# Turning K with VectorE's 32x32 block transposes, loaded one head per 32 partitions, in a decode attention kernel

## The chip, the cores and the metric

The kernel runs on one core of a Trainium2 chip. The metric is device time in microseconds (us) for one execution. Before the change it is 199.75 us (median of 3 runs, 199.69 to 199.76).

## What is computed

A layer norm of x (8 rows of 512) feeds two branches. One is decode attention with 32 query heads over 8 KV heads; only the last W = 2048 of 8192 cache positions count. The other is a gated MLP. The result is x + attention * silu(MLP).

```python
B, Sq, D = 8, 1, 512
Hq, Hkv, Sk, Dh = 32, 8, 8192, 128          # W = 2048, rep = Hq // Hkv = 4
q = (xn @ wq).reshape(B, Sq, Hq, Dh)
k = repeat(k_cache[:, :, Sk - W:, :], rep);  v = repeat(v_cache[:, :, Sk - W:, :], rep)
p = softmax(einsum("bhqd,bhkd->bhqk", q, k) * Dh ** -0.5)
s = einsum("bhqk,bhkd->bhqd", p, v).reshape(B, Sq, Hq * Dh) @ wo
g = silu((sigmoid(xn @ w_gate) * (xn @ w_up)) @ w_down)      # w_gate, w_up: 512 x 1792
return x + s * g
```

All tensors are bf16. K and V of the window are 33.55 MB each; wq and wo 4.19 MB each; the three MLP weights 1.84 MB each.

## The kernel before

**Tiles.** A unit of work is one tile of K or V: one batch and a group of GL = 4 KV heads, so NT = 16 tiles of each. A tile is 128 partitions x 64 positions x 128 of head dimension in bf16, 2 MB, 16 KB contiguous per partition. Line 109 (`load_kv`) loads it in one transfer, with the four heads interleaved: partition 4p + j holds head j, positions 64p to 64p + 63. K and V use the same function.

**Transfers.** All bulk loads go out on SP's queue (line 87), into a ring of RING = 9 buffers of equal size; wq takes two of them at first. The list `loads` (line 137) orders the tiles by the slot that needs them: K tile i at slot 4i, V tile i at slot 4i + PV_LAG, with PV_LAG = 11. The three MLP weights stand before the last two V tiles, and wo comes last. `issue_loads` issues as many as there are free buffers; each issue waits on SP for the former user of its buffer.

**Slots.** The order of work is written by hand (line 597). A slot t is a quarter of a K tile (16 of its 64 positions per partition, CC = 16); there are 8 slots for a batch and 64 in all. `k_half` (line 406) runs twice a slot. It reads K as 32-bit words (two neighbouring bf16 of the head dimension) and turns 128x128 words on TensorE against a 32-bit identity, four to a PSUM bank (line 415); VectorE copies the bank to `kT_sb` in SBUF and sorts the four heads apart on the way (line 419). So after every second slot, `kT_sb` holds 64 word indices x 2 positions on its partitions. `qk` (line 423) then makes the scores: 2 halves of the word (e) x 4 heads, each head a product with 32 columns of weights in its own 32 columns of the array (line 434), summed over the batch's 8 slots into one PSUM bank. The query weights come from `qz_sb` (line 262), a zero padded tile; the window that a product reads from it puts the queries in the rows that belong to the slot.

**Queries.** `q_projection` (line 348) makes q in two halves, with the head dimension's even and odd members apart; ScalarE copies it to bf16 (line 369), VectorE turns 32x32 blocks (line 371) and places it into `qz_sb` with 32 copies of 32 elements (line 376).

**Softmax and PV.** Once a batch: row maximum (446), exponent on ScalarE (460), a VectorE block transpose (474), a permutation by TensorE (480) that brings the probabilities from head-major to the interleaved order of V's partitions, a copy, four masked copies (496), and the denominator (518, 520). `pv` (line 525) follows PV_LAG slots behind with 8 products a slot, and a sum for each tile (557, 564). At the end come the MLP (line 629), the output product with wo (line 647), gate and residual.

Of the kernel before, what the change touches and what calls it, by code (L numbers as in the profile page):

```python
# [10 lines left out]
def kernel(  # L11
# [13 lines left out]
    nc = tc.nc  # L25
    P = 128
    B, _, D = A_x.shape
    _, Hkv, Sk, Dh = A_k_cache.shape
    Hq = A_wq.shape[1] // Dh
    rep = Hq // Hkv  # L30
# [4 lines left out]
    win0 = Sk - W  # L35
# [2 lines left out]
    ALIGN = 512  # L38


    GL = 4
    NG = Hkv // GL
    PP = P // GL
    CH = W // PP
    NJ = 4
    CC = CH // NJ
    HALF = CC // 2
    NX = NG * NJ
    XR = NX * rep
    NT = B * NG  # L50
    SPB = NG * NJ
    NSLOT = B * SPB
    PV_LAG = SPB + 3

    D2 = Dh // 2
    NJ2 = NJ // 2
    QB = 2 * rep
    QPAD = XR - QB
    RING = 9
    NCOL = 2  # L60
    DC = D // NCOL

    bf16 = mybir.dt.bfloat16
    f32 = mybir.dt.float32
# [6 lines left out]
    consts = ctx.enter_context(tc.tile_pool(name="consts", bufs=1))  # L71
    work = ctx.enter_context(tc.tile_pool(name="work", bufs=1))
    small = ctx.enter_context(tc.tile_pool(name="small", bufs=2))
    ring = ctx.enter_context(tc.tile_pool(name="ring", bufs=RING))
    ktpool = ctx.enter_context(tc.tile_pool(name="ktpool", bufs=2))
    ppool = ctx.enter_context(tc.tile_pool(name="ppool", bufs=2))
    psum = ctx.enter_context(
        tc.tile_pool(name="psum", bufs=2, space=bass.MemoryType.PSUM)
# [8 lines left out]
    def load(dst, src, q=None):  # L87
        if q is None:
            q = nc.sync
        q.dma_start(out=dst, in_=src)  # L90

    def ring_tile(shape, name):
        return ring.tile(shape, bf16, name=name, tag="ring", align_bytes=ALIGN)
# [5 lines left out]
    KH = KT // 2  # L99
    wq_sb = []  # L100
# [5 lines left out]
    k_tiles = {}  # L106
    v_tiles = {}

    def load_kv(cache, i, name):
        b, gg = divmod(i, NG)  # L110
        t = ring_tile([P, CH, Dh], name)
        load(
            t[:].rearrange("p c d -> p (c d)"),
            cache[b, GL * gg : GL * (gg + 1), win0:Sk, :].rearrange(
                "j (p c) d -> p j (c d)", c=CH
            ),
        )
        return t

    wg_sb = []  # L120
# [42 lines left out]
    def issue_loads():  # L163
        while loads_done[0] < len(loads) and free_bufs[0] > 0:
            kind, i = loads[loads_done[0]]
            if kind == 0:
                k_tiles[i] = load_kv(A_k_cache, i, "k_sb")
            elif kind == 1:
                v_tiles[i] = load_kv(A_v_cache, i, "v_sb")
            elif kind == 2:  # L170
                load_mlp(i)
            else:
                load_wo(i)
            loads_done[0] += 1
            free_bufs[0] -= 1
# [10 lines left out]

    ident = consts.tile([P, P], bf16, name="ident")
    make_identity(nc, ident[:])
    identf = consts.tile([P, P], f32, name="identf")
    make_identity(nc, identf[:])  # L190
    SumM = consts.tile([P, P], f32, name="SumM")
    nc.gpsimd.memset(SumM[:], 0.0)
    for off in range(-rep * (NJ - 1), rep * NJ, rep):
# [64 lines left out]

    QW = 3 * QPAD + 2 * QB
    qz_sb = work.tile([P, B, Hkv, QW], bf16, name="qz_sb")
    nc.vector.memzero(qz_sb[:])


# [32 lines left out]
    FQ = F // 4  # L298
# [2 lines left out]
    gate = work.tile([NCOL * 32, DC], f32, name="gate")  # L301

    def unit_in(w_sb):
        d_ps = psum.tile([P, FQ], f32, name="d_ps", tag="kT_ps")
        for kt in range(KT):
            for c in range(4):
                nc.tensor.matmul(
                    d_ps[32 * c : 32 * (c + 1), :],
                    lhsT=xnT_sb[:, kt, :],
                    rhs=w_sb[:, kt, FQ * c : FQ * (c + 1)],  # L310
                    start=(kt == 0),
                    stop=(kt == KT - 1),
                    tile_position=(0, 32 * c),
                    skip_group_check=True,
                )
        d_tiles.append(d_ps)
# [29 lines left out]


    def q_projection():
        HH = Hq // 2
        q_ps = [  # L350
            psum.tile([P, HH, 32], f32, name=f"q_ps{hh}", tag="kT_ps") for hh in range(2)
        ]
        for kt in range(KT):
            for hh in range(2):
                for c in range(4):
                    nc.tensor.matmul(  # L356
                        q_ps[hh][32 * c : 32 * (c + 1), :, :],
                        lhsT=xnT_sb[:, kt, :],
                        rhs=wq_sb[kt // KH][:, kt % KH, :].rearrange(
                            "p (h a m e) -> p h a m e", a=2, m=32, e=2  # L360
                        )[:, HH * hh : HH * (hh + 1), c % 2, :, c // 2],
                        start=(kt == 0),
                        stop=(kt == KT - 1),
                        tile_position=(0, 32 * c),
                        skip_group_check=True,
                    )
        for hh in range(2):
            q_sb = ppool.tile([P, HH * 32], bf16, name="q_sb", tag="p_bf")
            nc.scalar.copy(out=q_sb[:], in_=q_ps[hh][:].rearrange("p h m -> p (h m)"))
            qT_sb = ppool.tile([P, HH * 32], bf16, name="qT_sb", tag="pt_bf")  # L370
            nc.vector.transpose(out=qT_sb[:], in_=q_sb[:])  # L371
            GH = Hkv // 2
            for e in range(2):
                for c2 in range(2):
                    for r in range(rep):
                        nc.vector.tensor_copy(  # L376
                            out=qz_sb[
                                D2 * c2 : D2 * (c2 + 1),
                                :,
                                GH * hh : GH * (hh + 1),  # L380
                                QPAD + (QB + QPAD) * e + rep * c2 + r,
                            ],
                            in_=qT_sb[D2 * e : D2 * (e + 1), :].rearrange(
                                "p (g r b) -> p r b g", r=rep, b=32
                            )[:, r, :B, :],
                        )

    q_projection()
    free_bufs[0] += 2
# [10 lines left out]
    acc_sbs = {}  # L400
    oT_sb = work.tile([P, B, Hq], bf16, name="oT_sb")

    CP = CC // 2
    HP = CP // 2

    def k_half(t, h2):
        kw = k_tiles[t // NJ][:].rearrange("p (u c) d -> p u (c d)", c=2).bitcast(f32)
        u0 = (t % NJ) * CP + h2 * HP  # L410
        if t % 2 == 0 and h2 == 0:
            kT_tiles[t // 2] = ktpool.tile([P, 2 * CP, GL, PP], f32, name="kT_sb")
        kT_ps = psum.tile([P, HP, P], f32, name="kT_ps")
        for uu in range(HP):
            nc.tensor.transpose(  # L415
                out=kT_ps[:, uu, :], in_=kw[:, u0 + uu, :], identity=identf[:, :]
            )
        o0 = (t % 2) * CP + h2 * HP
        nc.vector.tensor_copy(  # L419
            out=kT_tiles[t // 2][:, o0 : o0 + HP, :, :],  # L420
            in_=kT_ps[:].rearrange("p u (k gl) -> p u gl k", gl=GL),
        )

    def qk(n):
        i, j2 = divmod(n, NJ2)
        b, gg = divmod(i, NG)
        x = NJ2 * gg + j2
        if x == 0:
            s_tiles[b] = psum.tile([P, CC * PP], f32, name="s_ps")
        kT = kT_tiles.pop(n)[:].bitcast(bf16).rearrange("p u gl (k e) -> p u gl k e", e=2)  # L430
        for e in range(2):
            z0 = QPAD + (QB + QPAD) * e - QB * x
            for gl in range(GL):
                nc.tensor.matmul(  # L434
                    s_tiles[b][XR * gl : XR * (gl + 1), :],
                    lhsT=qz_sb[:, b, GL * gg + gl, z0 : z0 + XR],
                    rhs=kT[:, :, gl, :, e],
                    start=(x == 0 and e == 0),
                    stop=(x == NG * NJ2 - 1 and e == 1),
                    tile_position=(0, XR * gl),  # L440
                    skip_group_check=True,
                )

# [33 lines left out]
    def soft_permute(b):  # L477

        pT_ps = psum1.tile([P, CC * XR], f32, name="pT_ps", tag="pT_ps")
        nc.tensor.matmul(  # L480
            pT_ps[:],
            lhsT=perm[:],
            rhs=pt_tiles.pop(b)[:].rearrange("k (u x w) -> k x u w", x=NX // 2, w=QB),
            start=True,
            stop=True,
        )
        pc_bf = ppool.tile([P, CC * XR], bf16, name="pc_bf")
        nc.scalar.copy(out=pc_bf[:], in_=pT_ps[:])  # L488
        pc_tiles[b] = pc_bf
# [107 lines left out]
    for t in range(NSLOT + PV_LAG):  # L597
# [1 line left out]
        b, ph = t // SPB - 1, t % SPB  # L599
        in_b = 0 <= b < B  # L600
        if t < NSLOT:
            k_half(t, 0)
        if in_b and ph == 3:
            soft_mask(b)
            dh_of[b] = soft_den_part(b)
        if t < NSLOT:
            k_half(t, 1)
        if in_b and ph == 2:
            soft_turn(b)
        if 0 < t <= NSLOT and t % 2 == 0:  # L610
            qk(t // 2 - 1)
        if in_b and ph == 0:
            mj_of[b] = soft_max_part(b)
        if in_b and ph == 1:
# [25 lines left out]
    o_rows(1)  # L640


    a_ps = psum.tile([NCOL * 32, DC], f32, name="a_ps", tag="kT_ps")
    order = [(hg, j) for hg in range(HG) for j in range(4)]
    for n, (hg, j) in enumerate(order):
        for c in range(NCOL):
# [48 lines left out]
```

## Time and profile before

| what | before |
|---|---|
| median of 3 runs | 199.75 us |
| the profiled execution | 199.84 us |
| its span, first to last instruction | 198.1 us |
| TensorE busy | 145.6 us, 73% |
| weight loads busy | 99.7 us, 50% |
| VectorE busy | 125.3 us, 63% |
| ScalarE busy | 22.9 us, 12% |
| GpSimd busy | 9.0 us, 5% |
| moved by DMA | 81.26 MB, 410 GB/s over the span |
| issue to landing, K tile and V tile (median) | 32.2 us and 34.9 us |

Engine times overlap, and their shares are means over the whole span. A group of instructions in the profile has its line, engine, operation, output and input tile, shapes and count; then busy time in us, the mean of one in ns; then the engine's idle time just before them and what ended most of it. The DMA share is the mean over the core's 16 DMA engines. Times on TensorE are modelled from start to end and overlap, so the mean of one product is longer than the distance between two.

### The profile page before, as it was taken

How to read it: one execution, taken by the hardware profiler on the slowest of the kernel's cores; microseconds unless marked ns; L12 is line 12 of the kernel's file. 1: busy time of each engine (PE TensorE's matmuls, PEld its weight loads, DVE VectorE, ACT ScalarE, POOL GpSimd, SP SyncE). 2: the span in 40 equal slices, each digit the busy share in tenths (PEclk: the TensorE clock that was granted, in tenths of full speed). 3: DMA queues.
4: the chain of work that ended last, by engine and by line, in shares of the span. 5: the costliest groups of instructions: out<-in, count | busy, mean ns of one | idle time of the engine just before them, and what ended most of it. 6: DMA issues, size and time to landing. Idle time of an engine off the chain costs nothing.

```text
span 198.1 us, 3706 instructions
## 1 busy us (share of the span) xinstructions
PE 145.6 (73%) x1576; PEld 99.7 (50%) x1576; DVE 125.3 (63%) x280; ACT 22.9 (12%) x48; POOL 9.0 (5%) x22
## 2 busy tenths in 40 slices
PE   0073599839997996969696879786949797746682
PEld 0023455526755764657564656564636565325471
DVE  2808867966797788847775867577627787134111
ACT  2001000040021002001100200030000300610000
POOL 7910000000000000000000000000000000000000
PEclk9999999996999999997999979997885999797579
DMA  6999999999999999999999999999999999999970
GB/s 213 425 433 437 440 430 422 423 423 440 433 433 430 427 423 430 427 437 427 433 427 422 437 430 433 427 430 427 427 430 433 431 428 428 435 423 413 418 306 15
DMA packets 6720, 81.26 MB, mean 410 GB/s; under 512 B 776, under 2 KB 816, under 8 KB 1968
## 3 DMA queue, kind: packets, MB, share of 16 engines
q1 hardware_dynamic: 6608, 81.01, 96.3%
q8 instruction: 12, 0.20, 0.4%
q14 instruction: 4, 0.03, 0.0%
q0 software_dynamic: 64, 0.01, 0.0%
q10 hardware_dynamic: 32, 0.01, 0.0%
HBM read 81.02 MB, written 0.01 MB: 409 GB/s over the span
## 4 chain that ended last, share of the span: by engine, by line
DMA 62%; PE 24%; DVE 10%; ACT 1%; issue 1%; SPq 0%; ACTq 0%
DMA k_sb<-in_A_k_cache_dram 31%; DMA v_sb<-in_A_v_cache_dram 18%; PE kT_ps L415 15%; DMA wo_sb<-in_A_wo_dram 7%; DMA wq_sb<-in_A_wq_dram 6%; PE s_ps L434 4%; DVE kT_sb L419 4%; PE acc_ps L536 3%; DVE qz_sb L376 2%; DVE pT_sb L496 1%; PE q_ps L356 1%; DVE qT_sb L371 1%; DVE pt_bf L474 1%; ACT L460 1%; PE den_ps L518 1%
## 5 line engine op out<-in xcount | busy, mean ns | idle before, releaser
L419 DVE COPY kT_sb<-kT_ps 128x512 f32<-128x512 f32 x128 | 83.8, 687 | 34.4 <-PE kT_ps L415 32.5
L415 PE MATMUL kT_ps<-identf,k_sb 128*128 128x128 f32 x512 | 79.1, 300 | 15.0 <-DMA k_sb<-in_A_k_cache_dram 11.3
L415 PEld LDWEIGHTS kT_ps<-identf,k_sb 128*128 128x128 f32 x512 | 61.9, 153 | 38.6 <-issue 20.6
L536 PE MATMUL acc_ps<-v_sb,pT_sb 128*32 128x256 bf16 x512 | 26.8, 298 | 9.5 <-DVE pT_sb L496 8.1
L434 PE MATMUL s_ps<-kT_sb,qz_sb 128*32 128x512 bf16 x256 | 21.9, 422 | 0.3 <-DVE kT_sb L419 0.3
L536 PEld LDWEIGHTS <-pT_sb 128*32 128x32 bf16 x512 | 11.6, 100 | 19.5 <-DVE pT_sb L496 9.0
L549 ACT COPY acc_sb<-acc_ps 128x256 f32<-128x256 f32 x16 | 5.9, 372 | 70.5 <-PE acc_ps L536 70.5
L460 ACT ACTIVATE p_bf<-s_ps,nm 128x512 bf16<-128x512 f32 x8 | 5.5, 687 | 46.4 <-DVE nm L457 46.4
L557 PE MATMUL oT_ps<-Sel,acc_sb 128*128 128x16 f32 x64 | 9.4, 261 | 2.0 <-ACT acc_sb L549 1.1
L557 PEld LDWEIGHTS oT_ps<-Sel,acc_sb 128*128 128x128 f32 x64 | 9.2, 208 | 3.2 <-ACT acc_sb L549 2.0
L496 DVE TENSOR_SCALAR pT_sb<-pc_bf,Hm 128x512 bf16<-128x512 bf16 x32 | 9.0, 346 | 0.0
L480 PE MATMUL pT_ps<-pt_bf,perm 128*128 128x512 bf16 x8 | 3.2, 403 | 7.4 <-DVE pt_bf L474 7.4
L290 PE MATMUL xnT_ps<-ident,xn_bf 8*128 8x8 bf16 x4 | 0.3, 175 | 9.6 <-DVE xn_bf L280 9.6
L434 PEld LDWEIGHTS <-qz_sb 128*32 128x32 bf16 x256 | 4.1, 97 | 6.5 <-issue 6.5
L474 DVE STREAM_TRANSPOSE pt_bf<-p_bf 128x512 bf16<-128x512 bf16 x8 | 5.6, 704 | 1.7 <-ACT p_bf L460 1.7
L647 PE MATMUL a_ps<-wo_sb,o_sb 128*32 128x256 bf16 x64 | 5.5, 329 | 0.9 <-DMA wo_sb<-in_A_wo_dram 0.9
L446 DVE TENSOR_REDUCE mx<-s_ps 128x1 f32<-128x512 f32 x8 | 5.5, 685 | 1.1 <-PE s_ps L434 0.9
L520 DVE RECIPROCAL rden<-den_ps 128x32 f32<-128x32 f32 x8 | 2.9, 358 | 4.4 <-PE den_ps L518 4.4
L194 POOL TENSOR_SCALAR_AFFINE_SELECT SumM<-SumM 128x128 f32<-128x128 f32 x7 | 5.4, 772 | 0.5
L488 ACT CAST pc_bf<-pT_ps 128x512 bf16<-128x512 f32 x8 | 4.7, 585 | 6.4 <-PE pT_ps L480 6.4
L647 PEld LDWEIGHTS <-o_sb 128*32 128x32 bf16 x64 | 4.3, 117 | 1.9 <-issue 1.5
L564 DVE TENSOR_TENSOR oT_sb<-oT_ps,rden 128x16 bf16<-128x16 f32 x16 | 2.7, 166 | 4.0 <-PE oT_ps L557 4.0
(63 smaller groups left out, 60.0 us busy)
## 6 DMA issues: line engine op xcount, KB each, us to landing
k_sb<-in_A_k_cache_dram SPq DMA_DIRECT2D x16, 2048.0 KB, 32.2
v_sb<-in_A_v_cache_dram SPq DMA_DIRECT2D x16, 2048.0 KB, 34.9
wq_sb<-in_A_wq_dram SPq DMA_DIRECT2D x2, 2048.0 KB, 9.7
wo_sb<-in_A_wo_dram SPq DMA_DIRECT2D x2, 1024.0 KB, 31.4
wg_sb<-in_B_w_gate_dram SPq DMA_DIRECT2D x1, 1792.0 KB, 34.0
wu_sb<-in_B_w_up_dram SPq DMA_DIRECT2D x1, 1792.0 KB, 36.4
wd_sb<-in_B_w_down_dram SPq DMA_DIRECT2D x1, 1792.0 KB, 31.3
wo_sb<-in_A_wo_dram SPq DMA_DIRECT2D x3, 512.0 KB, 24.1
```

The costliest lines, as they stand in the source:

```text
L194: nc.gpsimd.affine_select(out=SumM[:], in_=SumM[:], compare_op=ALU.not_equal, fill=1.0, base=-off, pattern=[[-1, P]], channel_multiplier=1,)
L415: nc.tensor.transpose(out=kT_ps[:, uu, :], in_=kw[:, u0 + uu, :], identity=identf[:, :])
L419: nc.vector.tensor_copy(out=kT_tiles[t // 2][:, o0 : o0 + HP, :, :], in_=kT_ps[:].rearrange("p u (k gl) -> p u gl k", gl=GL),)
L434: nc.tensor.matmul(s_tiles[b][XR * gl : XR * (gl + 1), :], lhsT=qz_sb[:, b, GL * gg + gl, z0 : z0 + XR], rhs=kT[:, :, gl, :, e], start=(x ...
L446: nc.vector.reduce_max(out=mx[:], in_=s_tiles[b][:], axis=AX.X)
L460: nc.scalar.activation(out=p_bf[:], in_=s_tiles.pop(b)[:], func=AF.Exp, bias=nm[:], scale=scale, accum_out=den128[:],)
L474: nc.vector.transpose(out=pt_bf[:], in_=p_bf[:])
L496: nc.vector.tensor_scalar(out=pT_tiles[b][:, :, gl, :], in0=pc, scalar1=Hm[:, gl : gl + 1], scalar2=None, op0=ALU.mult,)
L536: nc.tensor.matmul(acc_tiles[i][32 * c : 32 * (c + 1), :], lhsT=pT_tiles[b][:, x * (CC // 2) + n, :, :].rearrange("p g n -> p (g n)"), rhs ...
L549: nc.scalar.copy(out=acc_sb[:], in_=acc_tiles.pop(i)[:])
L557: nc.tensor.matmul(oT_ps[:], lhsT=acc_sb[:, Dh * c2 : Dh * (c2 + 1)], rhs=Sel[:].rearrange("p (g c r) -> p c g r", g=GL, c=2)[:, c2], star ...
L647: nc.tensor.matmul(a_ps[32 * c : 32 * (c + 1), :], lhsT=o2_sb[:, hg, j, :], rhs=wo_parts[hg, j][:, DC * c : DC * (c + 1)], start=(n == 0), ...
```

## The change

- `load_kv` is split. V is loaded as before. A K tile is loaded by four transfers, one for each head: head j goes to partitions 32j to 32j + 31, 16 KB contiguous per partition as before.
- `k_half` (TensorE transposes into PSUM, VectorE evictions) becomes `k_turn`: one VectorE transpose for a slot, straight from the K tile to `kT_sb`, 128 partitions x 1024 words of 32 bits, in blocks of 32x32. The second identity goes. `ktpool` has 3 buffers of one slot instead of 2 of two slots.
- On a partition of `kT_sb` there now stands one word index (of 32) of one head; the four heads lie in the four groups of 32 partitions, and the head dimension's 64 words are two blocks (a) of 32. `qk` runs every slot with 4 products (a and e), each with 128 columns of weights: a column belongs to one head, and its weights are zero on the other heads' partitions.
- `qz_sb` is laid out for that: 9,984 elements per partition instead of 5,632. `q_projection` puts one KV head in each 32 partitions, ScalarE's copy sorts even and odd members apart, and VectorE places the result with 8 copies instead of 32.
- The permutation's input is read in another order (line 483), since positions are sorted by slot now.

```diff
@@ -38,13 +38,13 @@
     CC = CH // NJ
-    HALF = CC // 2
     NX = NG * NJ
@@ -52,10 +52,10 @@
-    D2 = Dh // 2
-    NJ2 = NJ // 2
-    QB = 2 * rep
-    QPAD = XR - QB
+    NA = Dh // (2 * PP)
+    QPAD = XR - rep
+    QW = QPAD + P
     RING = 9
@@ -72,7 +72,7 @@
     ring = ctx.enter_context(tc.tile_pool(name="ring", bufs=RING))
-    ktpool = ctx.enter_context(tc.tile_pool(name="ktpool", bufs=2))
+    ktpool = ctx.enter_context(tc.tile_pool(name="ktpool", bufs=3))
     ppool = ctx.enter_context(tc.tile_pool(name="ppool", bufs=2))
@@ -106,15 +106,27 @@
-    def load_kv(cache, i, name):
+    def load_v(i):
         b, gg = divmod(i, NG)
-        t = ring_tile([P, CH, Dh], name)
+        t = ring_tile([P, CH, Dh], "v_sb")
         load(
             t[:].rearrange("p c d -> p (c d)"),
-            cache[b, GL * gg : GL * (gg + 1), win0:Sk, :].rearrange(
+            A_v_cache[b, GL * gg : GL * (gg + 1), win0:Sk, :].rearrange(
                 "j (p c) d -> p j (c d)", c=CH
...
         )
+        return t
+    def load_k(i):
+        b, gg = divmod(i, NG)
+        t = ring_tile([P, CH, Dh], "k_sb")
+        for gl in range(GL):
+            load(
+                t[PP * gl : PP * (gl + 1), :, :].rearrange("p c d -> p (c d)"),
+                A_k_cache[b, GL * gg + gl, win0:Sk, :].rearrange(
+                    "(p c) d -> p (c d)", c=CH
+                ),
+            )
         return t
@@ -164,9 +176,9 @@
             if kind == 0:
-                k_tiles[i] = load_kv(A_k_cache, i, "k_sb")
+                k_tiles[i] = load_k(i)
             elif kind == 1:
-                v_tiles[i] = load_kv(A_v_cache, i, "v_sb")
+                v_tiles[i] = load_v(i)
             elif kind == 2:
@@ -186,8 +198,6 @@
     make_identity(nc, ident[:])
-    identf = consts.tile([P, P], f32, name="identf")
-    make_identity(nc, identf[:])
     SumM = consts.tile([P, P], f32, name="SumM")
@@ -258,8 +268,7 @@
-    QW = 3 * QPAD + 2 * QB
-    qz_sb = work.tile([P, B, Hkv, QW], bf16, name="qz_sb")
+    qz_sb = work.tile([P, B, NG, NA * 2, QW], bf16, name="qz_sb")
     nc.vector.memzero(qz_sb[:])
@@ -301,7 +310,7 @@
     def unit_in(w_sb):
-        d_ps = psum.tile([P, FQ], f32, name="d_ps", tag="kT_ps")
+        d_ps = psum.tile([P, FQ], f32, name="d_ps", tag="wide")
         for kt in range(KT):
@@ -346,44 +355,39 @@
     def q_projection():
-        HH = Hq // 2
+        HW = rep * Dh
         q_ps = [
-            psum.tile([P, HH, 32], f32, name=f"q_ps{hh}", tag="kT_ps") for hh in range(2)
+            psum.tile([P, HW], f32, name=f"q_ps{gg}", tag="wide") for gg in range(NG)
         ]
         for kt in range(KT):
-            for hh in range(2):
-                for c in range(4):
+            for gg in range(NG):
+                for gl in range(GL):
+                    h0 = HW * (GL * gg + gl)
                     nc.tensor.matmul(
-                        q_ps[hh][32 * c : 32 * (c + 1), :, :],
+                        q_ps[gg][32 * gl : 32 * (gl + 1), :],
                         lhsT=xnT_sb[:, kt, :],
-                        rhs=wq_sb[kt // KH][:, kt % KH, :].rearrange(
-                            "p (h a m e) -> p h a m e", a=2, m=32, e=2
-                        )[:, HH * hh : HH * (hh + 1), c % 2, :, c // 2],
+                        rhs=wq_sb[kt // KH][:, kt % KH, h0 : h0 + HW],
                         start=(kt == 0),
                         stop=(kt == KT - 1),
-                        tile_position=(0, 32 * c),
+                        tile_position=(0, 32 * gl),
                         skip_group_check=True,
                     )
-        for hh in range(2):
-            q_sb = ppool.tile([P, HH * 32], bf16, name="q_sb", tag="p_bf")
-            nc.scalar.copy(out=q_sb[:], in_=q_ps[hh][:].rearrange("p h m -> p (h m)"))
-            qT_sb = ppool.tile([P, HH * 32], bf16, name="qT_sb", tag="pt_bf")
+        for gg in range(NG):
+            q_sb = ppool.tile([P, HW], bf16, name="q_sb", tag="p_bf")
+            nc.scalar.copy(
+                out=q_sb[:].rearrange("p (y e w) -> p y e w", e=2, w=PP),
+                in_=q_ps[gg][:].rearrange("p (y w e) -> p y e w", e=2, w=PP),
+            )
+            qT_sb = ppool.tile([P, HW], bf16, name="qT_sb", tag="pt_bf")
             nc.vector.transpose(out=qT_sb[:], in_=q_sb[:])
-            GH = Hkv // 2
-            for e in range(2):
-                for c2 in range(2):
-                    for r in range(rep):
-                        nc.vector.tensor_copy(
-                            out=qz_sb[
-                                D2 * c2 : D2 * (c2 + 1),
-                                :,
-                                GH * hh : GH * (hh + 1),
-                                QPAD + (QB + QPAD) * e + rep * c2 + r,
-                            ],
-                            in_=qT_sb[D2 * e : D2 * (e + 1), :].rearrange(
-                                "p (g r b) -> p r b g", r=rep, b=32
-                            )[:, r, :B, :],
-                        )
+            for gl in range(GL):
+                c0 = QPAD + XR * gl
+                nc.vector.tensor_copy(
+                    out=qz_sb[PP * gl : PP * (gl + 1), :, gg, :, c0 : c0 + rep],
+                    in_=qT_sb[PP * gl : PP * (gl + 1), :].rearrange(
+                        "p (r y b) -> p b y r", r=rep, b=32
+                    )[:, :B],
+                )
@@ -400,44 +404,34 @@
-    CP = CC // 2
-    HP = CP // 2
-    def k_half(t, h2):
-        kw = k_tiles[t // NJ][:].rearrange("p (u c) d -> p u (c d)", c=2).bitcast(f32)
-        u0 = (t % NJ) * CP + h2 * HP
-        if t % 2 == 0 and h2 == 0:
-            kT_tiles[t // 2] = ktpool.tile([P, 2 * CP, GL, PP], f32, name="kT_sb")
-        kT_ps = psum.tile([P, HP, P], f32, name="kT_ps")
-        for uu in range(HP):
-            nc.tensor.transpose(
-                out=kT_ps[:, uu, :], in_=kw[:, u0 + uu, :], identity=identf[:, :]
-            )
-        o0 = (t % 2) * CP + h2 * HP
-        nc.vector.tensor_copy(
-            out=kT_tiles[t // 2][:, o0 : o0 + HP, :, :],
-            in_=kT_ps[:].rearrange("p u (k gl) -> p u gl k", gl=GL),
-        )
-    def qk(n):
-        i, j2 = divmod(n, NJ2)
+    def k_turn(t):
+        i, j = divmod(t, NJ)
+        kT_tiles[t] = ktpool.tile([P, CC, NA, PP], f32, name="kT_sb")
+        nc.vector.transpose(
+            out=kT_tiles[t][:].rearrange("p c a k -> p (c a k)"),
+            in_=k_tiles[i][:, CC * j : CC * (j + 1), :]
+            .rearrange("p c d -> p (c d)")
+            .bitcast(f32),
+        )
+    def qk(t):
+        i, j = divmod(t, NJ)
         b, gg = divmod(i, NG)
-        x = NJ2 * gg + j2
+        x = NJ * gg + j
         if x == 0:
             s_tiles[b] = psum.tile([P, CC * PP], f32, name="s_ps")
-        kT = kT_tiles.pop(n)[:].bitcast(bf16).rearrange("p u gl (k e) -> p u gl k e", e=2)
-        for e in range(2):
-            z0 = QPAD + (QB + QPAD) * e - QB * x
-            for gl in range(GL):
+        z0 = QPAD - rep * x
+        kT = kT_tiles.pop(t)[:].rearrange("p c a k -> p (c a k)").bitcast(bf16)
+        kT = kT.rearrange("p (c a k e) -> p c a k e", a=NA, k=PP, e=2)
+        for a in range(NA):
+            for e in range(2):
                 nc.tensor.matmul(
-                    s_tiles[b][XR * gl : XR * (gl + 1), :],
-                    lhsT=qz_sb[:, b, GL * gg + gl, z0 : z0 + XR],
-                    rhs=kT[:, :, gl, :, e],
-                    start=(x == 0 and e == 0),
-                    stop=(x == NG * NJ2 - 1 and e == 1),
-                    tile_position=(0, XR * gl),
+                    s_tiles[b][:],
+                    lhsT=qz_sb[:, b, gg, 2 * a + e, z0 : z0 + P],
+                    rhs=kT[:, :, a, :, e],
+                    start=(x == 0 and a == 0 and e == 0),
+                    stop=(x == NX - 1 and a == NA - 1 and e == 1),
                     skip_group_check=True,
@@ -480,7 +474,7 @@
             lhsT=perm[:],
-            rhs=pt_tiles.pop(b)[:].rearrange("k (u x w) -> k x u w", x=NX // 2, w=QB),
+            rhs=pt_tiles.pop(b)[:].rearrange("k (c y r) -> k y c r", y=NX, r=rep),
             start=True,
@@ -599,16 +593,14 @@
         if t < NSLOT:
-            k_half(t, 0)
+            k_turn(t)
         if in_b and ph == 3:
...
             dh_of[b] = soft_den_part(b)
-        if t < NSLOT:
-            k_half(t, 1)
         if in_b and ph == 2:
             soft_turn(b)
-        if 0 < t <= NSLOT and t % 2 == 0:
-            qk(t // 2 - 1)
+        if 0 < t <= NSLOT:
+            qk(t - 1)
         if in_b and ph == 0:
@@ -640,7 +632,7 @@
-    a_ps = psum.tile([NCOL * 32, DC], f32, name="a_ps", tag="kT_ps")
+    a_ps = psum.tile([NCOL * 32, DC], f32, name="a_ps", tag="wide")
     order = [(hg, j) for hg in range(HG) for j in range(4)]
...
         for c in range(NCOL):
```

## The prediction

> **What bounds the kernel now.** I read the slices first. Each of the 40 is 5 us of the 198.1 us span; a digit is the busy share in tenths.
>
> ```profile
> PE   0073599839997996969696879786949797746682
> ...
> DVE  2808867966797788847775867577627787134111
> ...
> DMA  6999999999999999999999999999999999999970
> GB/s 213 425 433 437 440 430 422 423 423 440 433 433 430 427 423 430 427 437 427 433 427 422 437 430 433 427 430 427 427 430 433 431 428 428 435 423 413 418 306 15
> ```
>
> DMA is full from the second slice to the last but two; no engine is. So the end is set by the bytes divided by the pace of the queue, and compute matters only where it starves the queue or trails it. The queue table and the chain of waits that ended last agree:
>
> ```profile
> q1 hardware_dynamic: 6608, 81.01, 96.3%
> ...
> DMA 62%; PE 24%; DVE 10%; ACT 1%; issue 1%; SPq 0%; ACTq 0%
> ```
>
> One queue carries 81.01 MB and is busy for 96.3% of the span. Next, what that pace depends on. Windows of the trace (stretch, its length, busy time of PE, weight loads, VectorE, ScalarE, GpSimd, PE clock, DMA share, GB/s):
>
> ```profile
> 3.00:12.00 9.00, 2.14 (x20) 0.79 (x21) 5.56 (x14) 0.29 (x1) 6.98 (x14) 1.00 1.01 431
> ...
> 50.00:130.00 80.00, 67.71 (x778) 47.93 (x776) 59.89 (x124) 8.80 (x21) 0.00 (x0) 0.96 1.01 430
> ...
> 160.00:172.00 12.00, 9.63 (x128) 5.84 (x130) 7.28 (x14) 2.27 (x6) 0.00 (x0) 0.94 1.00 427
> ```
>
> The first stretch is wq alone, with compute nearly idle; the second is K and V with PE and VectorE busy; in the third the MLP weights come too. The pace is 427 to 431 each time. It is therefore a limit of the transfer itself, one that neither compute nor the tensor moves. What all these transfers have in common is that each writes 128 partitions. The change takes this away from K.
>
> **The change, part by part.** First the stream. The listing of transfers has K as 16 x 2048.0 KB, 33.55 MB; at 430 GB/s that is 78.0 us, 4.88 us for a tile. After the change a tile is four transfers, each of one head into 32 partitions. No bulk transfer of the trace writes fewer than 128, so the price is bounded from both sides. Lower end: the limit sits in the 16 DMA engines, they all work on any transfer, and K still takes 78.0 us (a gain is a rival below). Upper end: the limit sits where SBUF is written, in proportion to partitions, and transfers of one queue do not overlap; a quarter of the partitions then moves at a quarter of the pace, and K takes 312.0 us, 234 more. I choose twice, 156.0 us, **+78.0 us**: the geometric middle, because neither end has a row of its own. The windows' flat pace speaks for a limit of fixed width, hence against no loss at all; but a DMA engine with 2 rows of each head instead of 8 rows of a tile can run on into the next head's partitions before its neighbours have finished, hence against four times.
>
> The Trainium skill, page "SBUF — State Buffer", section "Door 1: The DMA port swizzle (why `[64,N]` ≈ `[32,N]`)", says partitions 0 to 31 reach 8 of 16 write ports, with 189 GB/s measured at 1 MiB against 328 for all 128, and an asymptote of about 218; an estimate from that figure gives K 33.55 MB / 218 GB/s = 153.9 us, and so 275.7 us for the whole. Its next section, "Can I just issue two DMAs to hit both halves?", says that transfers to different halves serialize, which speaks against this change. No row here shows either.
>
> The issuing: 48 more on SP's queue, at the 535 ns median of a K issue, are 25.7 us of SP time. Nothing computes there, and each waits for its ring buffer anyway: the waits on SP's queue that start with PE's release of K and V buffers are 102.6 us (53.6 + 49.0). Behind a K issue stand the next V issue and, late, the weights; issue to landing is a median 32.2 us, so the queue holds over six tiles (32.2 / 4.88) as cover. Cost 0; with the cover gone, 3 x 0.535 = 1.6 us for each of 16 tiles.
>
> The turning. Out: 512 transposes on TensorE and their 128 evictions. In: 64 VectorE block transposes, each 128 partitions x 1024 words. The rows to price them by:
>
> ```profile
> L419 DVE COPY kT_sb<-kT_ps 128x512 f32<-128x512 f32 x128 | 83.8, 687 | 34.4 <-PE kT_ps L415 32.5
> L415 PE MATMUL kT_ps<-identf,k_sb 128*128 128x128 f32 x512 | 79.1, 300 | 15.0 <-DMA k_sb<-in_A_k_cache_dram 11.3
> ...
> L434 PE MATMUL s_ps<-kT_sb,qz_sb 128*32 128x512 bf16 x256 | 21.9, 422 | 0.3 <-DVE kT_sb L419 0.3
> ...
> L474 DVE STREAM_TRANSPOSE pt_bf<-p_bf 128x512 bf16<-128x512 bf16 x8 | 5.6, 704 | 1.7 <-ACT p_bf L460 1.7
> ...
> L480 PE MATMUL pT_ps<-pt_bf,perm 128*128 128x512 bf16 x8 | 3.2, 403 | 7.4 <-DVE pt_bf L474 7.4
> L446 DVE TENSOR_REDUCE mx<-s_ps 128x1 f32<-128x512 f32 x8 | 5.5, 685 | 1.1 <-PE s_ps L434 0.9
> ```
>
> A reduce over 512 costs 685 ns and one over 4 (line 457) 154, so an element is (685 - 154) / 508 = 1.045 ns. By elements a turn is 704 + 512 x 1.045 = 1,239 ns, 64 are 79.3 us against 83.8 removed. By bytes (4,096 against 1,024 a partition) it is 4 x 704 = 2,816 ns, 180.2 us. I take 1.24 us: the row is the same operation and PSUM evictions of 4-byte words cost no more an element. VectorE's other work is, for each batch of 8 slots, 4 x 0.346 + 0.704 + 0.685 + 0.358 + 2 x 0.166 + 0.234 + 0.230 + 0.154 = 4.08 us, 0.51 a slot. A slot (a quarter K tile, a quarter V tile) streams in 2 x 4.88 / 4 = 2.44 us, 3.66 with K at half pace. So 1.75 us (up to 3.33) is hidden under 3.66: cost 0.
>
> The products. 256 as before, but with 128 columns of weights, no longer four side by side. A slot had 8 transposes (1.02 us in the chain of waits) and half of 8 products (0.62 us for eight in the order of time): 1.33 us. Now 4 products: at 0.31 (two rounds of four took 0.62) 1.24 us, at line 480's 403 ns 1.61. The dearer one plus PV's eight (0.40) and the softmax's share (some 0.28) is 2.29, hidden under either stream; I take it: 0.
>
> The front. The zeroing of the query tile (line 263, 2.405 us for 2,816 words) grows to 4,992 words, +1.86 us. It stands ahead of the layer norm on VectorE, so the first half of the q products starts at 12.0 instead of 10.15 and ends at 13.9, and the second, which began at 13.11 on wq's landing, is 0.8 later. ScalarE's two copies now write in another order: 0.54 each, or up to 1.6 times that by line 325's strided block transpose (980 ns for 448 elements). VectorE then makes 8 copies instead of 32, of 128 elements each: 0.14 + 96 x 1.045 ns = 0.24 us, 1.9 against 4.4. q is ready near 19.5, not 21.2. At half pace K's first tile lands 4.9 later than the 18.0 of the first transpose, so turning starts near 23. This is no term of its own: the buffers that wq frees 0.8 later are needed only behind five queued tiles. Two GpSimd steps for the second identity go, off the path. The third kT buffer only adds room.
>
> The tail. Behind the last K come V, the three MLP weights, the last two V and wo, all over 128 partitions and unchanged: 0.
>
> Sum: 198.1 + 78.0 = 276.1 us of span. The profiled execution took 199.84 us, 1.7 outside its span; the median of the runs is 199.75, 0.09 below it. **Forecast: 278 us** (277.8 rounded).
>
> **The rivals.** *Pace unchanged, and not slower.* The mechanism: four heads' transfers are in flight on one queue, all 128 partitions are being written at any time, and each transfer reads one stretch of 512 KB. For it: the queue is never short of work. Price: with nothing gained, 199.8; if the shorter stride of reading lifts K to the best slice's 440 GB/s, K takes 76.3 and the time is 198.1. It decides from K at 432 GB/s, which gives 0.4 us. Against it: 440 appears in slices, never in a long window. The skill's second section above is against it too.
>
> *VectorE becomes the bound*, at unchanged pace. Start 21, 64 slots, then some 30 us from the last turn when everything has landed (16.3 from 166.6 to 182.9 on the timeline, 2 for the last PV, 5.5 for the output product, the rest the small steps and the end of the span). It overtakes the stream when 21 + 64 s + 30 exceeds 198.1: s above 2.30, a turn above 1.79 us. At 2.82 the time is 21 + 213 + 30 + 1.7 = 266; at twice the row, 2.48, 244. At half pace it needs a turn above 3.0 us, over the upper end.
>
> *Partial overlap.* Two neighbouring heads half cover each other: K at 1.3 to 1.7 times, 223 to 254.
>
> *Worse than half.* If DMA engines drift apart, V's writes collide with K's as well; a quarter of V's 78.0 on top gives about 298, and the full quarter pace 434.
>
> *The change does not relieve VectorE*, though it says it replaces TensorE's turning: 79.3 against 83.8 is hardly less. This moves no term while the stream decides.
>
> **How the numbers follow.** K at about half pace, 262 to 300: 0.65. Partial overlap or VectorE, 205 to 262: 0.15. Above 300: 0.05. Pace unchanged: 0.15, of which 0.08 faster and 0.07 the same. The main case gets most since it needs only that the flat pace belongs to the written partitions, and both neighbours of it lie on the same side. The likeliest case's own range is 262 to 300; the 80% range takes in the middle cases, 205 to 300. A measurement of this kernel tells about 0.2% (0.4 us) from no change. Faster 0.08, same 0.07, slower 0.85.
>
> **What would show it.** In the changed profile: GB/s near 215 in stretches where K lands, alternating to 430 for V, so slices near 290; a DMA share still full; K tiles 9.8 us apart from V's 4.9; VectorE's turn 1.2 us and TensorE idle for long. Wrong if the slices stay at 430 (the limit is in the DMA engines), if a turn takes over 1.8 us with VectorE at nine tenths, or if the queue idles between heads.

## The result, and the profile after

The changed kernel takes 318.46 us (median of 4 runs, 312.88 to 321.34) against 199.75 before: 1.576 times as long, interval 1.571 to 1.581. On another chip it took 315.32 (311.57 to 330.52), 1.567 times, 1.560 to 1.573. These ratios and intervals use only the runs within 1.5% of the kernel's fastest, so they are a little under the ratio of the medians. It is slower, as forecast, but by 119 us instead of 78, outside the range. The kernel before stays within 0.3 us on one chip, this one spreads over 19; that is part of the story below. The profile shown is of the run of 321.34 us, its span 319.6.

The slices of the changed kernel are 8 us each:

```profile
PE   0406647533726270627365181734707256095575
...
DVE  4455553604441351407160260605414072053221
...
DMA  7999999999999999999999999999999999999930
GB/s 297 351 207 219 207 351 207 329 215 314 207 316 217 289 213 291 211 281 209 242 238 219 254 212 240 215 240 207 225 228 224 232 219 279 366 433 421 396 125 13
```

DMA is as full as before, at 254 GB/s on average over the span against 410. A full share here says that the DMA engines always had a packet in hand, not that it moved at pace. In the first half of the run slices near 210 alternate with slices of 280 to 350; in the second half, up to the last K near 279 us, nearly all are 207 to 254; then 433 and 421 are back. Its queue table and chain of waits:

```profile
q1 hardware_dynamic: 7376, 81.01, 95.8%
...
DMA 98%; SPq 0%; DVE 0%; issue 0%; PE 0%
DMA k_sb<-in_A_k_cache_dram 65%; DMA v_sb<-in_A_v_cache_dram 28%; DMA wo_sb<-in_A_wo_dram 5%; SPq L90 0%; DVE prod L649 0%; DVE y_bf L651 0%; PE a_ps L639 0%
```

The bytes are the same 81.01 MB; compute has left the chain. The groups of instructions that replace the turning on TensorE, and the zeroing:

```profile
L429 PE MATMUL s_ps<-kT_sb,qz_sb 128*128 128x512 bf16 x256 | 95.3, 514 | 122.6 <-DVE kT_sb L410 122.6
L410 DVE STREAM_TRANSPOSE kT_sb<-k_sb 128x1024 f32<-128x1024 f32 x64 | 76.4, 1218 | 144.8 <-DMA k_sb<-in_A_k_cache_dram 144.8
...
L272 DVE MEMSET qz_sb<- 128x4992 uint32 x1 | 4.2, 4218 | 1.0 <-issue 1.0
```

VectorE's turn takes 1,218 ns, and VectorE stands idle 144.8 us for K's landings; the products stand 122.6 us for VectorE. Nothing here is short of compute.

Now K and V apart. Each transfer raises its semaphore 16 times, once for each DMA engine, and the trace has the time of every one. From these, for the V tiles of this run: when the last engine was through, how long after the last engine of the transfer ahead, the same interval for the mean of the 16 engines, and how far the first and the last engine lay apart.

```
V tile landed (us)  after the one ahead (us)  by the mean engine (us)  first to last engine (us)
  47.89               4.92                      4.96                     0.51
  65.49               7.64                      5.36                     3.25
 100.47               8.21                      6.24                     7.04
 135.82               9.45                      6.91                     9.51
 190.95               9.67                      8.02                    12.92
 267.20               9.61                      9.01                    14.87
```

By the mean engine a head of K takes 2.27 to 2.66 us throughout, 2.46 on average, that is 0.524 MB at some 213 GB/s. V's first tile behind heads takes the 4.9 us of before. Then the DMA engines come out of step, from half a microsecond to 15 (16.7 in the last heads of K), and V's tiles come to take nearly twice as long. The first step, from 0.62 to 3.25 us, comes with two packets of program code on other queues (at 58.12 and 59.99 us, 1.07 and 0.32 us long); the next, to 5.53 us at the V tile of 83.29 us, has no such packet, so the stream widens the gap by itself. That the code packets start it is argued from these times alone.

Windows of the same trace (columns as in the prediction):

```profile
28.20:38.04 9.84, 5.29 (x19) 1.89 (x18) 4.62 (x4) 0.00 (x0) 0.00 (x0) 0.85 1.01 213
42.97:47.89 4.92, 3.50 (x10) 1.47 (x9) 4.51 (x6) 1.13 (x1) 0.00 (x0) 0.50 1.09 410
...
219.15:228.66 9.51, 6.94 (x35) 2.83 (x34) 7.60 (x14) 1.74 (x4) 0.00 (x0) 0.63 1.02 225
228.66:238.31 9.65, 2.04 (x22) 0.89 (x23) 0.00 (x0) 0.00 (x0) 0.00 (x0) 0.73 1.00 222
```

First four heads of K at 213 GB/s, then the first such V tile at 410; late in the run the stretches that end with a V tile's and with four heads' last landing, at 225 and 222. By then the engines lie over 13 us apart, so each of these two stretches holds packets of both K and V. Single packets say it without that mixing. A packet of 16 KB takes 611 ns in the kernel before (50 to 130 us). Here, from 200 to 260 us, the median is 1,207 ns, and of 816 packets, K's and V's together, none is under 700. The engines are at work all the time; each packet takes twice as long, V's too.

The sum, from the landings of both kernels (us): the time up to the landing of wq, the intervals of K's and of V's transfers up to the last K, and the rest of the span.

| | before, last engine | after, last engine | before, mean engine | after, mean engine |
|---|---|---|---|---|
| up to wq | 13.1 | 13.3 | 12.9 | 13.0 |
| K, 16 tiles | 80.3 | 152.1 | 78.6 | 157.5 |
| V, 13 tiles | 63.7 | 113.3 | 63.3 | 95.7 |
| behind the last K | 41.1 | 40.8 | 43.3 | 53.4 |
| span | 198.1 | 319.6 | 198.1 | 319.6 |

The span grew by 121.5. How this divides depends on the engine that is followed: the last one falls back in V's tiles and makes some of it good in K's heads. By the last engine K costs 71.8 more and V 49.7; by the mean engine K 78.9 and V 32.4, and another 10.1 stand behind the last K, where the mean engine is done 12.6 us ahead of the last one. It isn't only the longest runs: in the trace of 309.07 us below, V's 13 tiles take 101.7 by the last engine and 88.1 by the mean.

### The profile page after: what moved, and what is told of

It is laid out like the page before. It is cut to its first block, busy times and chain, and to the rows that moved or that the text cites. A ratio compares the mean times of both kernels' runs of the same rounds, so it can differ in the third digit from the quotient of the medians.

```text
span 319.6 us, 2653 instructions
## 1 busy us (share of the span) xinstructions
PE 151.8 (47%) x1064; PEld 63.3 (20%) x1064; DVE 117.0 (37%) x192; ACT 22.7 (7%) x48; POOL 10.6 (3%) x20
## 3 DMA queue, kind: packets, MB, share of 16 engines
q1 hardware_dynamic: 7376, 81.01, 95.8%
## 4 chain that ended last, share of the span: by engine, by line
DMA 98%; SPq 0%; DVE 0%; issue 0%; PE 0%
DMA k_sb<-in_A_k_cache_dram 65%; DMA v_sb<-in_A_v_cache_dram 28%; DMA wo_sb<-in_A_wo_dram 5%; SPq L90 0%; DVE prod L649 0%; DVE y_bf L651 0%; PE a_ps L639 0%
## 5 line engine op out<-in xcount | busy, mean ns | idle before, releaser
L429 PE MATMUL s_ps<-kT_sb,qz_sb 128*128 128x512 bf16 x256 | 95.3, 514 | 122.6 <-DVE kT_sb L410 122.6
L410 DVE STREAM_TRANSPOSE kT_sb<-k_sb 128x1024 f32<-128x1024 f32 x64 | 76.4, 1218 | 144.8 <-DMA k_sb<-in_A_k_cache_dram 144.8
L429 PEld LDWEIGHTS <-qz_sb 128*128 128x128 bf16 x256 | 27.6, 119 | 169.4 <-issue 159.6
L530 PE MATMUL acc_ps<-v_sb,pT_sb 128*32 128x256 bf16 x512 | 31.8, 344 | 22.0 <-DMA v_sb<-in_A_v_cache_dram 21.4
L530 PEld LDWEIGHTS <-pT_sb 128*32 128x32 bf16 x512 | 9.5, 103 | 46.7 <-issue 25.3
L551 PEld LDWEIGHTS oT_ps<-Sel,acc_sb 128*128 128x128 f32 x64 | 10.1, 206 | 5.3 <-ACT acc_sb L543 2.0
L204 POOL TENSOR_SCALAR_AFFINE_SELECT SumM<-SumM 128x128 f32<-128x128 f32 x7 | 7.3, 1037 | 0.5
L449 PEld LDWEIGHTS mb_ps<-mj,SumM 128*128 128x128 f32 x16 | 5.0, 314 | 3.6 <-issue 2.0
L474 PE MATMUL pT_ps<-pt_bf,perm 128*128 128x512 bf16 x8 | 4.2, 524 | 2.6 <-DVE pt_bf L468 2.6
L272 DVE MEMSET qz_sb<- 128x4992 uint32 x1 | 4.2, 4218 | 1.0 <-issue 1.0
L512 PE MATMUL den_ps<-dh,ones 128*128 128x32 f32 x16 | 3.9, 331 | 0.0
## 6 DMA issues: line engine op xcount, KB each, us to landing
wg_sb<-in_B_w_gate_dram SPq DMA_DIRECT2D x1, 1792.0 KB, 32.4
```

The lines of the kernel that those rows point to most:

```text
L204: nc.gpsimd.affine_select(out=SumM[:], in_=SumM[:], compare_op=ALU.not_equal, fill=1.0, base=-off, pattern=[[-1, P]], channel_multiplier=1,)
L410: nc.vector.transpose(out=kT_tiles[t][:].rearrange("p c a k -> p (c a k)"), in_=k_tiles[i][:, CC * j : CC * (j + 1), :] .rearrange("p c d ...
L429: nc.tensor.matmul(s_tiles[b][:], lhsT=qz_sb[:, b, gg, 2 * a + e, z0 : z0 + P], rhs=kT[:, :, a, :, e], start=(x == 0 and a == 0 and e == 0 ...
L449: nc.tensor.matmul(mb_ps[:], lhsT=SumM[:], rhs=mj[:], start=True, stop=True)
L530: nc.tensor.matmul(acc_tiles[i][32 * c : 32 * (c + 1), :], lhsT=pT_tiles[b][:, x * (CC // 2) + n, :, :].rearrange("p g n -> p (g n)"), rhs ...
L551: nc.tensor.matmul(oT_ps[:], lhsT=acc_sb[:, Dh * c2 : Dh * (c2 + 1)], rhs=Sel[:].rearrange("p (g c r) -> p c g r", g=GL, c=2)[:, c2], star ...
```

## The experiments

Three questions: is it K's transfers or the compute; what about these transfers is slow; and where does V's loss come from.

**K in one transfer again**, under the new compute.

```diff
-        for gl in range(GL):
-            load(
-                t[PP * gl : PP * (gl + 1), :, :].rearrange("p c d -> p (c d)"),
...
+        load(
+            t[:].rearrange("p c d -> p (c d)"),
+            A_k_cache[b, GL * gg : GL * (gg + 1), win0:Sk, :].rearrange(
+                "j (p c) d -> p j (c d)", c=CH
+            ),
+        )
```

> The changed kernel with K loaded as before, one transfer of a tile into 128 partitions with the heads interleaved; all its compute stays (the scores are then of mixed heads, so its output is not the reference's). Theory A, the loss is all in K's transfers: the stream is back at 430 GB/s and the time is 199 to 201 us, with VectorE's turn still 1.2 us. Rival, part of the loss is compute (turning on VectorE, products with 128 weight columns): over 205 us.

Measured: 198.44 us (198.3 to 198.5), 0.994 times before, interval 0.992 to 0.995. Its slices of 4.9 us, and its turning:

```profile
span 196.8 us, 2585 instructions
...
DMA  6999999999999999999999999999999999999990
GB/s 215 428 430 440 430 436 430 440 426 425 426 430 423 433 440 426 433 426 433 433 426 423 433 433 433 436 433 423 430 426 431 426 428 426 435 429 421 414 374 23
...
L409 DVE STREAM_TRANSPOSE kT_sb<-k_sb 128x1024 f32<-128x1024 f32 x64 | 76.4, 1218 | 32.2 <-DMA k_sb<-in_A_k_cache_dram 31.8 <-PE s_ps L428 0.3
```

With the same turning, products, zeroing and q placement the stream is back at some 430 and the whole loss is gone. The compute of the change even gives 1.25 us (199.69 - 198.44), a little outside what was expected.

**The other way round**: the kernel before, with only its K loads made by head (the `load_k` of the change in place of `load_kv` for K).

> The kernel before with only its K loads changed: four transfers of a tile, one head into 32 neighbouring partitions; all compute of before stays (scores of mixed positions, output not the reference's). Theory A: 311 to 322 us, as the changed kernel. Rival, the compute of the change makes some of the loss: clearly under 311.

Measured: 309.07 us, 2 us under the expected stretch, with 512 transposes on TensorE and their evictions still there. Together with the run above: the loss is in the loads. A few us between this and the changed kernel can't be told from that kernel's own spread.

**Same number of transfers and partitions, but spread**: head j into partitions 4p + j.

```diff
-                t[PP * gl : PP * (gl + 1), :, :].rearrange("p c d -> p (c d)"),
+                t[gl::GL, :, :].rearrange("p c d -> p (c d)"),
```

> The changed kernel with K still in four transfers of one head and 32 partitions each, but into every fourth partition (head j into 4p + j) instead of 32 neighbouring ones; the scores are of mixed heads. Theory A1, what counts is which partitions a transfer reaches (neighbouring ones share a limited part of the write side): pace back to 430 GB/s, 199 to 203 us. Rival A2, what counts is the number of partitions or rows in a transfer, or the number of transfers: as the changed kernel, 300 to 322 us.

Measured: 198.6 us. The slices:

```profile
span 196.9 us, 2653 instructions
...
GB/s 218 428 429 436 429 436 426 439 424 433 426 426 423 429 426 436 426 429 429 439 433 426 428 426 429 429 424 433 426 429 426 433 433 425 434 431 421 409 382 28
```

Four transfers of one head and 32 rows each run at full pace. So neither their number, nor their size, nor the contiguous 512 KB that each reads costs anything; what costs is that the 32 partitions are neighbours.

**64 neighbouring partitions**, two transfers of a tile.

```diff
-        for gl in range(GL):
...
+        for n in range(2):
+            load(
+                t[64 * n : 64 * (n + 1), :, :].rearrange("p c d -> p (c d)"),
+                A_k_cache[b, GL * gg : GL * (gg + 1), win0:Sk, :].rearrange(
+                    "j (n p c) d -> n p j (c d)", n=2, c=CH
+                )[n],
+            )
```

> The changed kernel with K in two transfers of a tile, each into 64 neighbouring partitions (0 to 63, 64 to 127), heads interleaved; the scores are of mixed heads. Theory A1 with the pace in proportion to the partitions reached would put 32 at a quarter and 64 at half; the landings show 32 at half, 2.44 us a head, so by proportion from there 64 neighbouring partitions go at full pace: 199 to 203 us. Theory A1 with partitions p and p + 32 on the same write path: 64 are no better than 32, half pace, 275 to 322 us.

Measured: 282.52 us. Twice the partitions, and K is still at half pace: half of a tile lands in 4.9 us where the tiles are in step. Partitions 32 to 63 therefore add nothing to 0 to 31. The page "SBUF — State Buffer" of the Trainium skill, section "Door 1: The DMA port swizzle (why `[64,N]` ≈ `[32,N]`)", says that partitions 0 to 31 and 0 to 63 reach the same 8 of 16 ports; the traces agree, with 213 GB/s for 32 neighbours against the page's asymptote of about 218, and no more for 64.

**Both halves in flight at once**: heads 0 and 1 on SP's queue, 2 and 3 on ScalarE's; in a second kernel on GpSimd's, with `(nc.sync, nc.gpsimd)` for `queues`.

```diff
+                q=queues[gl // 2],
```

> The changed kernel with heads 0 and 1 of each K tile issued on SP's queue and heads 2 and 3 on ScalarE's, so that transfers to both halves of the partitions are in flight at the same time; nothing else differs. Theory A (two DMA engines that write the same path at once take turns, and each engine is held up by the packet it is writing): a second queue helps only as far as the engines happen to be on different halves, 250 to 322 us. Rival (the loss is that one queue works on one half at a time): both halves together reach the full pace, 199 to 210 us.

> The same with heads 2 and 3 on GpSimd's queue, whose transfers may be shared out over the DMA engines in another way. Theory A: 250 to 322 us. Rival, as in the run before: 199 to 210 us.

Measured: 330.21 and 312.02 us. With ScalarE's queue it is slower than most runs of the changed kernel and over the upper end by 8; with GpSimd's about equal. In the trace with ScalarE's queue, heads of the two queues, and so of the two halves, land by turns and still one in 2.4 us (30.59, 32.96 and 35.37 us). A second queue doesn't bring the full pace. The section "Can I just issue two DMAs to hit both halves?" on the same page of the Trainium skill says no, and the traces agree. ScalarE's queue has a cost beside that: its own work stands behind the K loads that it issues, as the order of time shows.

```profile
1.43 61.85 ACTq L90 DMA_DIRECT2D k_sb<-in_A_k_cache_dram  x10
63.32 1.28 ACT L285 ACT_TABLE_LOAD   x1 [63.32 <-DMA k_sb<-in_A_k_cache_dram]
```

The layer norm's step on ScalarE comes only behind these, at 64.6 us, and the first turn at 74.5 instead of 23.4. Whether this makes the 330 was not tried; the single runs of both kernels lie within the spread of the changed one.

**K without V.**

```diff
-                v_tiles[i] = load_v(i)
+                if i == 0:
+                    v_tiles[0] = load_v(0)
+                v_tiles[i] = v_tiles[0]
+                if i > 0:
+                    free_bufs[0] += 1
...
-        if u >= 0 and u % NJ == NJ - 1:
+        if u == NSLOT - 1:
             free_bufs[0] += 1
```

The lines on `free_bufs` keep the count of free buffers right.

> The changed kernel with V left out but for its first tile, which stands in for all 16 (73 us of stream less, output not the reference's). The changed kernel is some 40 us above K at half pace. Theory B, those 40 us arise between K's writes and V's when DMA engines are out of step: K alone is at exactly half pace, 2.44 us a head, its part 156 us, and the whole 199 to 208 us (the last K near 173, then the tail of the compute). Rival C, K's own transfers get slower than half in the long run: a head over 2.8 us on average, 222 us or more.

Measured: 214.05 us, between the two theories' ranges, so the total decides nothing. The chain of waits does (start, length, what):

```profile
78.11 19.89 DMA k_sb<-in_A_k_cache_dram
98.02 19.78 DMA k_sb<-in_A_k_cache_dram
117.82 19.34 DMA k_sb<-in_A_k_cache_dram
137.17 19.27 DMA k_sb<-in_A_k_cache_dram
156.46 19.24 DMA k_sb<-in_A_k_cache_dram
175.82 1.26 DVE kT_sb L414
```

Each piece is two tiles, eight heads: 19.24 to 19.89 us, 2.41 to 2.49 a head. K alone is at half pace to the end, and its engines come no further apart than 2.8 us. The miss is elsewhere: the last K is through at 175.8 instead of near 173, and from there to the end of the span at 212.3 it takes 36.5 us, where the expectation had some 30. Rival C falls.

**Six stops**, so that the engines start again in step.

```diff
+    scr = work.tile([1, 64], bf16, name="scr")
...
+            if kind == 0 and i % 2 == 1 and i > 3 and (i - 4) in v_tiles:
+                last = max(v_tiles)
+                nc.sync.dma_start(out=scr[:], in_=v_tiles[last][0:1, 0, :64])
```

> The changed kernel with six stops on SP's queue, one ahead of every second K tile from the sixth: a small copy out of the V tile issued last, so that all loads land before the next goes out and the DMA engines start again in step. Each stop costs 2 to 4 us of empty queue, 12 to 24 in all. Theory B (the 40 us come from engines that drift out of step): between stops K goes at 215 and V at 430 GB/s again, 287 on average, and the time falls in spite of the stops, 275 to 310 us. Rival D (V is slowed by K's shape whatever the step): no better between stops, 325 to 345 us.

> The changed kernel itself, beside the next run on the same chip. Its four runs lay between 312.9 and 321.3 us; theory B (drift that builds up differently in each run) expects again a spread of some us, 305 to 322, where the kernel before stays within 0.2 us.

> The changed kernel with the six stops, as before, to put an interval to it. Theory B: below every run of the changed kernel, 300 to 310 us, with a smaller spread since the drift is taken back six times. Rival D: not below it.

Measured: 306.51 us, and in the second round 306.19 (304.32 to 307.17), 1.532 times before, interval 1.527 to 1.537, against 1.560 to 1.573 for the changed kernel on that chip. The changed kernel's own spread, 311.57 to 330.52, was larger than expected; with stops it is 2.9. The slices with stops, 7.6 us each, in the second round:

```profile
span 304.8 us, 2664 instructions
...
DMA  7999999999599976999699967999699969999992
GB/s 299 357 209 219 213 290 262 302 247 258 170 206 342 206 277 140 245 310 267 213 206 344 209 275 173 284 275 301 186 230 310 215 234 241 340 421 438 410 418 112
```

The 5, the 6s and the 7s of the DMA row, but for its first digit, are the stops. Slices of 275 to 344 beside slices near 210, as early in the changed kernel, now come back to the end. In the landings, a first head comes 5.35 us after the last tile ahead of a stop (80.24 to 85.59) where 2.44 would do, so six stops cost some 6 x 2.9 = 17.5 us; right after a stop the engines are 0.2 to 0.6 us apart, and V tiles at 166.77, 200.89 and 215.74 us take 4.9 us. V's 13 tiles take 68.8 us by the last engine, against 113.3 without stops and 63.7 in the kernel before. The stops' own cost taken off, the stream is at 289, some 27 us better than the changed kernel beside it (315.3 - 288.7). Rival D falls.

**V in the same shape as K.**

```diff
     def load_v(i):
...
+        for gl in range(GL):
+            load(
+                t[PP * gl : PP * (gl + 1), :, :].rearrange("p c d -> p (c d)"),
+                A_v_cache[b, GL * gg + gl, win0:Sk, :].rearrange(
+                    "(p c) d -> p (c d)", c=CH
+                ),
+            )
```

> The changed kernel with V loaded like K, one head into 32 neighbouring partitions (V's heads then stand in other partitions than its products assume, output not the reference's). All of K and V is now of one shape. Theory E: the extra 40 us come from two shapes in one stream, in which an engine that is out of step writes into the other shape's way; with one shape only the half pace is left, 156 us for K and 156 for V, 198.1 + 2 x 78 + 1.7 = 356, so 345 to 362 us. Rival F, being out of step costs in any stream of 32 partition transfers: 375 us or more.

Measured: 357.6 us. The slices are 8.9 us:

```profile
span 355.9 us, 2725 instructions
...
GB/s 324 298 208 225 212 208 208 215 221 210 212 221 210 212 212 223 214 208 209 223 212 210 214 217 215 208 219 218 212 212 219 217 210 223 278 430 233 231 347 131
```

K and V now share one shape, both at half pace, and that is all: the term 2 x 78 fits to 2 us, and while K and V alternate the engines stay within 2.4 us of each other. So the loss above half pace, and the growing drift, belong to two shapes in one stream: of 32 neighbours and 128, here. Being out of step is not enough by itself: with 64 neighbours the engines also drift apart, to 10.0 us, and that kernel stays at 282.5, 5 over plain half pace. Why that mixture bears it and the one of 32 doesn't was not tried. Nor is it shown how one shape's packets slow the other's once the engines are out of step: the stops and the single shape show only that both together are needed.

Nothing here is a faster kernel to use: the two at 198.4 and 198.6 us have K in a layout that the block transposes don't fit, so their output is not the reference's.

## Why the prediction went wrong, step by step

- **What bounds the kernel** held: a stream at a pace set by what it writes, compute of no account.
- **K at twice its time** held: 152.1 us (last engine) to 157.5 (mean engine) measured against 156.0, and 2.41 to 2.49 us a head with K alone. That the sum had just this factor was luck: it was the middle of 1 and 4 times, without a mechanism that gives 2. The experiments show one: 32 neighbours reach half of what 128 reach, and 64 no more than 32. The estimate from ports that the prediction sets beside its sum (275.7) had it.
- **The step that failed is V's term: the sum put nothing on it.** The tail, "V, the three MLP weights, the last two V and wo, all over 128 partitions and unchanged: 0", held for what stands behind the last K. But 13 V tiles stand between K's, and 198.1 + 78.0 leaves them at their old 4.88 us because they are still 128 partitions wide. They rise to 9.0 us by the mean engine (9.6 by the last). The growth of 121.5 is 43.5 us over the 78.0: by the mean engine 32.4 in V and 10.1 in engines that fall behind. The mechanism stood among the rivals ("V's writes collide with K's as well") and was mis-sized there: a quarter of V, 19.5 us, to about 298, still inside the main case, while all above 300 had a chance of 0.05. Nothing in the trace of before could size it, since there only one shape flows.
- **The turning**: 1,218 ns, 76.4 us in all, against 1,239 and 79.3 by the row of elements. The price by bytes was far off, and the rival of VectorE as the bound is out: in the kernel with K back in one transfer VectorE is idle 32.2 us ahead of its turns.
- **The products**: four take 0.98 to 1.03 us in the chain of waits of the run without V, below both bounds (1.24 and 1.61). They are hidden either way.
- **The front**: zeroing 4.218 us against 4.27 worked out, the eight placing copies 2.1 against 1.9. Of no weight, as said.
- **The issuing** costs nothing; an issue of a head takes 0.311 us, not 0.535.
- **The compute as a whole** was put at 0; measured alone (K in one transfer) it gives 1.25 us. At the last K the mean engine is 0.3 us earlier than before, the last engine 1.35 (155.72 against 157.07), so most of the gain is in engines that are held back less. The program's own packets, 8 of 16 KB instead of 12, may be the reason; this was not taken apart.
- **Pace unchanged** was refuted in both its forms: heads in flight together don't cover each other, on one queue or two.
- **What would show it**: K near 215, a full DMA share and VectorE at 1.2 us came as written; "430 for V, so slices near 290" held only for the first V tiles, and no sign was named for V tiles that slow down.

## What to carry to other kernels

Before you split a load by partitions, ask which partitions each transfer reaches: 32 or 64 neighbours move at half the pace of 128, while the same 32 rows spread over every fourth partition cost nothing. When a narrow transfer shares a queue with full-width ones, price the others too: here the narrow one lost 72 to 79 us, and the others and the drift the remaining 43 to 50 of the 121.5. And a full DMA share is no pace; read it beside GB/s.

## What the runs showed of the hardware

- The 16 DMA engines of one queue are not kept in step. In the kernel before they stay within 3.6 us of each other over the whole run. With K in 32 neighbours and V in 128 they come 13.1, 16.7 and 20.1 us apart in the three traces with these loads, of 309.07, 321.34 and 330.52 us. That the drift makes the changed kernel's spread of 19 us fits these three and is not shown further.
- A stop that lets all loads land puts them back to 0.2 to 0.6 us, costs some 2.9 us, and can pay for itself (306.19 us with six of them against 315.32).
- The price of a block transpose on VectorE goes by elements, not bytes: 1,024 words of 32 bits take 1,218 ns, 512 of 16 bits 680 to 711.
